# First batch of a Fourier-filter and swish kernel: spectrum rows turned ahead of the tables, masks and beta arithmetic on GpSimd with the filter loads behind them, one filter half copied on chip

## The chip, the cores and the metric

The kernel runs on one core of one Trainium2 chip. The metric is the device time of one execution in microseconds (us). The experiments ran in several sets of rounds on different chips, each set with the kernel before beside it (its medians are 804.01 to 804.79 us, its spread in one set 0.2 to 1.0%), so a ratio is taken inside a set, and medians of different sets are compared with care. "A gain" below means that the 95% interval of the ratio lies under 1.

## The reference, cut to what matters

```python
def _attn_ref(x, filt_r, filt_i):              # x: (8, 3008, 256); filters: (1505, 256)
    X = np.fft.rfft(x, axis=1)
    F = (filt_r + 1j * filt_i)[None, :, :]
    y = np.fft.irfft(X * F, n=x.shape[1], axis=1)
    return y.astype(np.float32)

def _moe_ref(x, w_in, w_out, beta):            # x: (24064, 256); d_ff = 2048
    h = x @ w_in
    g = h * (1.0 / (1.0 + np.exp(-beta * h)))
    return (g @ w_out).astype(np.float32)

# out = _moe_ref(_attn_ref(x, filt_r, filt_i).reshape(24064, 256), w_in, w_out, beta)
```

## The kernel before: the parts that matter

The transforms are matrix products with small tables. A long loop of steps (one step is one block of 512 tokens and one of 16 slices of d_ff) does h, silu and the output product. The transforms of batches 1 to 7 are placed between its steps. Batch 0 has nothing to hide behind: its transform and the building of the tables are the set-up, and the loop starts when the first slice of batch 0 is done.

The set-up, cut. `gp` is GpSimd. VectorE (DVE) multiplies the spectrum by the filters; rows 0 to 63 of `fr_sb` hold the real filter and rows 64 to 127 the imaginary one.

```python
for g in range(NG):                                    # 4 groups of 6 frequencies
    load_filter(fr_sb, filt_r, 0, g * KG, KG, nc.sync)
for g in range(2):
    load_filter(fr_sb, filt_i, M, g * KG, KG, gp)      # two DMAs of 192 KB each
ws = [load_wout(i * WG, WG) for i in range(2)]         # output weights, 512 KB each, from SyncE
# ... cut: first table, ka, kb ...
angles(0, nc.vector)
m_p = bits("m_p", ip[:], ALU.bitwise_and, M - 1)       # keep: the mask of the row of frequency 0
# ... cut: three more small VectorE instructions for keep ...
angles(1, gp)                                          # u, r, u - r: 128 x 768 fp32 each
for g in range(2, NG):
    load_filter(fr_sb, filt_i, M, g * KG, KG, gp)
for h in range(WI):
    gp.dma_start(win_sb[:, :, fs], moe_w_in[:, fs].rearrange(...))
# ... cut: first1 (x times the first table), table3 and turn_a (PE transposes) ...

def product(i):
    # ... cut: matmuls into ps, two of each ...
    for dst, ps in zip((p_t, q_t), pss):
        nc.vector.tensor_tensor(dst[:], ps[:], fr_sb[:, 2 * i : 2 * i + 2, :], ALU.mult)
```

In the loop, batches 1 to 7 need a second filter tile and the real filter in the rows where batch 0 had the imaginary one:

```python
def uf():
    units = []
    for f_sb, filt, at in ((fi_sb, filt_i, 0), (fi_sb, filt_i, M), (fr_sb, filt_r, M)):
        units += load_filter(f_sb, filt, at, 0, NK, nc.scalar, True)   # six DMAs of 768 KB
    units.append(lambda: gp.tensor_scalar_mul(fi_sb[:, 0, :], fi_sb[:, 0, :], keep[:]))
    return units
```

Batch 1's spectrum goes through DRAM: tile `a` is written to `d` (d<-a) and read back turned (a<-d). The read is placed at step 20 and its first matmul at step 26.

Of the kernel before, what the change touches and what calls it, by code (L numbers as in the profile page):

```python
# [9 lines left out]
P = 128  # L10

ACT = mybir.ActivationFunctionType
ALU = mybir.AluOpType
# [11 lines left out]
M = 64  # L25
H = M // 2
NK = 24
J = 32
KG = 6
NG = NK // KG  # L30
# [6 lines left out]
def kernel(  # L37
# [10 lines left out]
    nc = tc.nc  # L48
# [7 lines left out]
    NDC = D // P  # L56
    NFB = FF // P
# [62 lines left out]
    def load_filter(f_sb, filt, at, k0, n, eng, later=False):  # L120
        lo = AP(filt.tensor, filt.offset + k0 * D, [[N1 * D, H], [1, n * D]])
        hi = AP(filt.tensor, filt.offset + (N1 - k0) * D, [[N1 * D, H], [-D, n], [1, D]])
        units = [
            lambda: eng.dma_start(
                f_sb[at : at + H, k0 : k0 + n, :].rearrange("p k d -> p (k d)"), lo
            ),
            lambda: eng.dma_start(f_sb[at + H : at + M, k0 : k0 + n, :], hi),
        ]
        if later:
            return units  # L130
        for go in units:
            go()

    def load_wout(f0, n):
        ws = ostp.tile([P, n, D], F32, name="ws", tag="ost")
        nc.sync.dma_start(
            ws[:], moe_w_out[f0 * P : (f0 + n) * P, :].rearrange("(fb fp) j -> fp fb j", fp=P)
        )
        return ws
# [11 lines left out]
    def small(name, dt=F32):  # L151
        return setup.tile([P, 1], dt, name=name, tag=name)
# [6 lines left out]
    def bits(name, src, op0, s0, op1=None, s1=None):  # L159
        shape = [P, src.shape[1]]  # L160
        ti = setup.tile(shape, I32, name=name + "_i", tag=name + "_i")
        if op1 is None:
            nc.vector.tensor_scalar(ti[:], src, s0, None, op0)
        else:
            nc.vector.tensor_scalar(ti[:], src, s0, s1, op0, op1)
        tf = setup.tile(shape, F32, name=name, tag=name)
        nc.vector.tensor_copy(tf[:], ti[:])
        return tf
# [6 lines left out]
    def warm(n, cols=512):  # L175
        for _ in range(n):
            nc.tensor.matmul(pw[0][:, :cols], lhsT=wz[:, :P], rhs=wz[:, :cols], start=True, stop=True)

    ip = setup.tile([P, 1], I32, name="ip", tag="ip")
# [16 lines left out]

    for g in range(NG):
        load_filter(fr_sb, filt_r, 0, g * KG, KG, nc.sync)
    for g in range(2):
        load_filter(fr_sb, filt_i, M, g * KG, KG, gp)  # L200

    WG = NFB // 4
    ws = [load_wout(i * WG, WG) for i in range(2)]

    pre = small("pre")
    nc.scalar.activation(pre[:], wz[:, :1], ACT.Silu)
# [56 lines left out]
    def t2_part(h, part):  # L263
        u, r = us[h], rs[h]
        ks_ = slice(h * NH, (h + 1) * NH)
        if part == 0:
            nc.scalar.activation(t2[:, ks_, 2, :], u[:], ACT.Sin, scale=TWO_PI)
        elif part == 1:
            nc.scalar.activation(r[:], u[:], ACT.Abs)
        else:  # L270
            for cols, sgn, b in ((slice(0, H), -1.0, hp), (slice(H, M), 1.0, hm)):
                nc.scalar.activation(
                    t2[:, ks_, 1, cols], r[:, :, cols], ACT.Sin, scale=sgn * TWO_PI, bias=b[:]
                )

    def t2_neg(h):
        ks_ = slice(h * NH, (h + 1) * NH)
        nc.vector.tensor_scalar_mul(t2[:, ks_, 4, :], t2[:, ks_, 1, :], -1.0)
        nc.vector.tensor_copy(t2[:, ks_, 0, :], t2[:, ks_, 1, :])
        nc.vector.tensor_copy(t2[:, ks_, 3, :], t2[:, ks_, 2, :])  # L280

    angles(0, nc.vector)
    m_p = bits("m_p", ip[:], ALU.bitwise_and, M - 1)
    nc.vector.tensor_scalar(keep[:], m_p[:], -1.0, float(M - 1), ALU.mult, ALU.add)
    nc.vector.tensor_tensor(keep[:], keep[:], m_p[:], ALU.mult)
    nc.vector.tensor_scalar(keep[:], keep[:], 0.5, None, ALU.is_gt)

    angles(1, gp)
    for g in range(2, NG):
        load_filter(fr_sb, filt_i, M, g * KG, KG, gp)  # L290
    WI = 4
    for h in range(WI):
# [6 lines left out]
    def first1(i, on_act):  # L299
        for dc in range(NDC):  # L300
            if dc:
                ps = opsum.tile([P, 4, P], F32, name="psa", tag="acc")
            else:
                ps = fpsum.tile([P, 4, P], F32, name="psa", tag="f")
            for e in range(4):
                nc.tensor.matmul(
                    ps[:, e, :KP],
                    lhsT=x_cur[:, 4 * i + e, dc * P : (dc + 1) * P],
                    rhs=t1b[:],
                    start=True,  # L310
                    stop=True,
                )
            evac(
                a_t[:, dc, :, 4 * i : 4 * i + 4, :].rearrange("p k j a -> p j k a"),
                ps[:, :, :KP].rearrange("p j (k a) -> p j k a", a=4),
                on_act[dc],
            )

    for i in range(3):
        first1(i, (True, True))  # L320
        warm(2)
    t2_part(0, 0)
    first1(3, (False, True))
    warm(2)
    t2_part(0, 1)
    first1(4, (False, False))
    warm(2)
    t2_part(0, 2)
    first1(5, (False, False))
    warm(2)  # L330
    for i in range(6, 8):
        first1(i, (False, True))
        warm(2)
    t2_neg(0)



    def table3(i, part, on_act):
        pt = opsum.tile([P, KG, P], BF16, name="pt", tag="acc")
        for e in range(KG):  # L340
            nc.tensor.transpose(
                pt[:, e, :],
                t2[:, KG * i + e, part : part + 2, :].rearrange("p c k -> p (c k)"),
                ident[:],
            )
        dst = t3 if part else t3b
        if i == 0:
            evac(dst[:, 0, :], pt[:, 0, :], on_act, 0.5)
            evac(dst[:, 1:KG, :], pt[:, 1:KG, :], on_act)
        else:  # L350
            evac(dst[:, KG * i : KG * i + KG, :], pt[:], on_act)
# [14 lines left out]
                )  # L366
        evac(a2s[-1][:, 3 * (i % 2) : 3 * (i % 2) + 3, :], pb[:], on_act)

    table3(0, 0, False)
    turn_a(0, True)  # L370
    turn_a(1, False)
    table3(0, 2, True)

    nc.vector.tensor_scalar_mul(fr_sb[M:P, 0, :], fr_sb[M:P, 0, :], keep[M:P])


    def beta_columns():
        bps = hpsum.tile([P, NFB], F32, name="bps", tag="hps")
        id_f = setup.tile([NFB, NFB], F32, name="id_f", tag="id_f")
        nc.vector.tensor_copy(id_f[:], ident[:NFB, :NFB])  # L380
        nc.tensor.transpose(bps[:], bt[:], id_f[:])
        tiny = setup.tile([P, NFB], F32, name="tiny", tag="tiny")
        nc.vector.tensor_copy(beta_sb[:], bps[:])
        nc.vector.tensor_tensor(tiny[:], beta_sb[:], beta_sb[:], ALU.mult)
        nc.vector.tensor_scalar(tiny[:], tiny[:], 1e-12, None, ALU.is_lt)
        nc.vector.scalar_tensor_tensor(
            beta_sb[:], tiny[:], 2e-6, beta_sb[:], ALU.mult, ALU.add
        )
        nc.vector.reciprocal(rbeta_sb[:], beta_sb[:])
        nc.vector.tensor_copy(  # L390
            t1.rearrange("p (a k) -> p a k", a=4), t1b.rearrange("p (k a) -> p a k", a=4)
        )

# [54 lines left out]
    for i in range(NK // 2 + 1):  # L448
        if i < NK // 2:
            product(i)  # L450
        if i % 3 < 2 and i // 3 < 3:
            turn_a(2 + 2 * (i // 3) + i % 3, True)
        if i % 3 > 0 and i // 3 < 3:
            table3(1 + i // 3, 4 - 2 * (i % 3), True)
        if i in (1, 2, 3):
            t2_part(1, i - 1)
        if i == 2:
            beta_columns()
        if i == 3:
            t2_neg(1)  # L460
        if i == 9:
            table4()
        if i > 0:
            inverse3(i - 1)
# [37 lines left out]
    def last_z(g, i, on_act):  # L502
        jq, dc = divmod(i, NDC)
        yv = ys[0][:, dc, g * CLS : (g + 1) * CLS].rearrange("p (n j) -> p n j", j=JG)
        last4(zz0[g], t4b, 4 * jq, dc, yv[:, :, 4 * jq : 4 * jq + 4], on_act)
# [143 lines left out]
    def u4(b, act=False):  # L649
        return [lambda i=i: s4(b, i, act and i % 2 == 1) for i in range(J // 2)]  # L650

    def uz(g):
        return [lambda i=i: turn_z(g, i) for i in range(2)] + [
            lambda i=i: last_z(g, i, False) for i in range(2 * NDC)
        ]

    def uf():
        units = []
        for f_sb, filt, at in ((fi_sb, filt_i, 0), (fi_sb, filt_i, M), (fr_sb, filt_r, M)):
            units += load_filter(f_sb, filt, at, 0, NK, nc.scalar, True)  # L660
        units.append(lambda: gp.tensor_scalar_mul(fi_sb[:, 0, :], fi_sb[:, 0, :], keep[:]))
        return units

    def ux(b):
# [3 lines left out]
        return [go]  # L668

    place(1, 13, uz(1))  # L670
    place(1, 7, uf(), per=2)
    place(15, 29, uz(2))
    place(34, 60, uz(3))

    first_step = [(S * b // TB) * NFB for b in range(B + 1)]
    if B > 1:
# [130 lines left out]
```

## Time and profile before

The median is 803.98 us (three runs, 803.89 to 806.82). The span of the profiled run is 801.5 us.

| what | before |
|---|---|
| first spectrum product on VectorE | 19.35 us |
| first matmul of the loop | 43.39 us |
| PE's wait for the read of batch 1's spectrum | 73.2 to 76.15 us |
| from the loop's first matmul to the end of the span | 758.1 us |

The page of the kernel before, first the engines' busy time (share of the span, instructions), then the ACT queue's DMAs (packets, MB, share of the engines). PE is TensorE's matmuls, PEld its weight loads, DVE VectorE, ACT ScalarE, POOL GpSimd:

```profile
PE 774.1 (97%) x6007; PEld 547.9 (68%) x6103; DVE 408.8 (51%) x670; ACT 589.0 (73%) x896; POOL 149.9 (19%) x148
...
q10 hardware_dynamic: 2496, 4.72, 2.7%
```

PE is busy 97% of the span, so little is to be gained outside the few places where it is not. 4.72 MB on the ACT queue are the six filter loads.

The timeline of the kernel before (start and duration in us, engine, line, operation, tiles; in brackets the idle time of the engine before it and what ended it), GpSimd and VectorE in the set-up:

```profile
6.64 0.59 POOL L124 DMA_DIRECT2D fr_sb<-in_filt_i_dram  x1
...
10.28 1.48 POOL L252 TENSOR_TENSOR u<-ka,kb 128x768 f32<-128x768 f32 x1
...
14.73 1.80 POOL L259 TENSOR_TENSOR u<-u,r 128x768 f32<-128x768 f32 x1
...
15.05 1.69 DVE L278 TENSOR_SCALAR t<-t 128x768 bf16<-128x768 bf16 x1
...
16.67 0.35 DVE L279 COPY t<-t 128x768 bf16<-128x768 bf16 x1
...
18.91 0.35 DVE L374 TENSOR_SCALAR fr_sb<-fr_sb,keep 64x256 f32<-64x256 f32 x1
...
19.35 0.69 DVE L418 TENSOR_TENSOR pb_t<-ps,fr_sb 128x512 bf16<-128x512 f32 x1
```

The first group of the imaginary filter is issued at 6.64 us, ahead of the angles (10.28 to 16.53 us). VectorE's negation took 1.69 us while GpSimd's last angle instruction ran; the same instruction took 0.36 us at its second use. The products start at 19.35 us.

The timeline of PE at the start of the loop and at the read, in the kernel before:

```profile
43.39 1.02 PE L735 MATMUL hps<-y,win_sb 128*128 128x512 bf16 x4
...
76.15 0.39 PE L567 MATMUL ps<-a,t 128*128 128x256 bf16 x2 [2.89 <-DMA a<-d]
```

The windows view of the kernel before around that read (stretch, its length, then busy us and count of instructions of PE, PE's weight loads, DVE, ACT and POOL, then granted PE clock, DMA share, GB/s):

```profile
77.00:79.00 2.00, 2.00 (x9) 1.08 (x8) 1.65 (x3) 0.69 (x1) 0.20 (x1) 0.59 0.94 352
79.00:81.00 2.00, 2.00 (x12) 1.18 (x10) 1.47 (x3) 0.69 (x1) 1.06 (x1) 0.55 0.17 68
81.00:84.00 3.00, 2.95 (x26) 2.12 (x25) 2.71 (x5) 2.06 (x3) 1.27 (x1) 1.00 0.00 0
```

PE waited 2.89 us for the read, and its granted clock (the share of full speed that TensorE was given) was 0.59 and 0.55 from 77 to 81 us.

### The profile page before, as it was taken

How to read it: one execution, taken by the hardware profiler on the slowest of the kernel's cores; microseconds unless marked ns; L12 is line 12 of the kernel's file. 1: busy time of each engine (PE TensorE's matmuls, PEld its weight loads, DVE VectorE, ACT ScalarE, POOL GpSimd, SP SyncE). 2: the span in 40 equal slices, each digit the busy share in tenths (PEclk: the TensorE clock that was granted, in tenths of full speed). 3: DMA queues.
4: the chain of work that ended last, by engine and by line, in shares of the span. 5: the costliest groups of instructions: out<-in, count | busy, mean ns of one | idle time of the engine just before them, and what ended most of it. 6: DMA issues, size and time to landing. Idle time of an engine off the chain costs nothing.

```text
span 801.5 us, 15281 instructions
## 1 busy us (share of the span) xinstructions
PE 774.1 (97%) x6007; PEld 547.9 (68%) x6103; DVE 408.8 (51%) x670; ACT 589.0 (73%) x896; POOL 149.9 (19%) x148
## 2 busy tenths in 40 slices
PE   7798999999999999999999999999999999999997
PEld 4665667776677667776678766687667766776664
DVE  8874965574527655375644655357462770500001
ACT  5855776787677866788667886778767788677775
POOL 8531520240003300042001310023100340000000
PEclk9999999999999999999999999999999999999999
DMA  9999459323932167211870119502280115010101
GB/s 175 229 226 262 97 152 223 111 91 102 221 107 74 66 156 189 95 48 66 196 217 28 67 68 216 175 28 92 98 233 27 71 69 124 32 49 28 54 27 52
DMA packets 85890, 93.01 MB, mean 116 GB/s; under 512 B 3745, under 2 KB 76978, under 8 KB 84970
## 3 DMA queue, kind: packets, MB, share of 16 engines
q1 hardware_dynamic: 80250, 72.37, 30.6%
q0 software_dynamic: 3072, 14.94, 9.9%
q10 hardware_dynamic: 2496, 4.72, 2.7%
q8 instruction: 47, 0.77, 0.4%
q14 instruction: 25, 0.20, 0.1%
HBM read 58.73 MB, written 46.66 MB: 131 GB/s over the span
## 4 chain that ended last, share of the span: by engine, by line
PE 85%; DMA 6%; DVE 3%; issue 2%; ACT 2%; POOL 1%; DVEq 0%; ACTq 0%; POOLq 0%; SPq 0%
PE acc L763 39%; PE hps L735 35%; PE ps L545 3%; DMA d<-a 3%; PE ps L493 3%; PE ps L567 2%; PE ps L594 2%; DMA fr_sb<-in_filt_r_dram 2%; DVE ost L775 1%; DMA a<-d 1%; DMA xg<-in_x_dram 1%; ACT z_t L105 1%; ACT a L105 0%; DVE p_t L577 0%; DVE q_t L581 0%
## 5 line engine op out<-in xcount | busy, mean ns | idle before, releaser
L744 ACT ACTIVATE gT<-hps,beta_sb 128x512 bf16<-128x512 f32 x752 | 516.4, 687 | 192.3 <-PE hps L735 162.3
L763 PE MATMUL acc<-wout_sb,gT 128*128 128x256 bf16 x3008 | 456.4, 273 | 5.6 <-DVE ost L775 2.0
L735 PE MATMUL hps<-y,win_sb 128*128 128x512 bf16 (+7 forms) x1634 | 428.6, 351 | 0.5 <-ACT gT L744 0.4
L763 PEld LDWEIGHTS <-gT 128*128 128x128 bf16 x3008 | 285.7, 98 | 135.0 <-issue 6.2
L735 PEld LDWEIGHTS <-win_sb 128*128 128x128 bf16 x1728 | 164.7, 98 | 25.5 <-issue 0.9
L584 POOL TENSOR_TENSOR v_t<-p_t,q_t 128x512 bf16<-128x512 f32 x84 | 106.6, 1269 | 367.7 <-DVE q_t L581 365.5
L775 DVE COPY ost<-acc 128x512 f32<-128x512 f32 x94 | 60.3, 683 | 193.7 <-PE acc L763 193.6
L107 DVE CAST a<-ps 96x512 bf16<-96x512 f32 x104 | 71.0, 686 | 80.0 <-PE ps L545 79.9
L109 DVE TENSOR_SCALAR y<-ps 128x376 bf16<-128x376 f32 x126 | 68.8, 548 | 69.3 <-PE ps L493 69.0
L577 DVE TENSOR_TENSOR p_t<-ps,fr_sb 128x512 f32<-128x512 f32 x84 | 58.1, 691 | 32.1 <-PE ps L567 30.7
L581 DVE TENSOR_TENSOR q_t<-ps,fi_sb 64x512 f32<-64x512 f32 x84 | 58.2, 693 | 1.2
L578 DVE SCALAR_TENSOR_TENSOR q_t<-ps,fi_sb 64x512 f32<-64x512 f32 x84 | 57.4, 684 | 1.1
L493 PEld LDWEIGHTS <-zz 96*128 96x128 bf16 x512 | 35.5, 98 | 29.3 <-issue 0.6
L105 ACT ACTIVATE z<-ps 128x512 bf16<-128x512 f32 x84 | 49.4, 588 | 0.3 <-PE ps L594 0.2
L545 PE MATMUL ps<-xg,t 94*96 94x512 bf16 x112 | 42.1, 381 | 0.6
L493 PE MATMUL ps<-t,zz 96*128 96x94 bf16 x448 | 36.8, 206 | 1.0
L567 PE MATMUL ps<-a,t 128*128 128x256 bf16 x168 | 32.4, 275 | 3.5 <-DMA a<-d 3.1
L594 PE MATMUL ps<-v_t,t 128*128 128x256 bf16 x168 | 32.1, 273 | 0.2
L116 POOL DMA_DIRECT2D xg<-in_x_dram x12 | 6.9, 579 | 120.4 <-PE acc L763 97.8
L567 PEld LDWEIGHTS <-t 128*128 128x128 bf16 x168 | 15.9, 98 | 18.0 <-DMA a<-d 3.0
L545 PEld LDWEIGHTS <-t 94*96 94x96 bf16 x112 | 13.8, 124 | 12.0
L594 PEld LDWEIGHTS <-t 128*128 128x128 bf16 x168 | 15.5, 98 | 7.9 <-DVE q_t L581 0.7
(115 smaller groups left out, 196.7 us busy)
## 6 DMA issues: line engine op xcount, KB each, us to landing
out_dram<-ost SPq DMA_DIRECT2D x41, 512.0 KB, 3.0
d<-a SPq DMA_DIRECT2D x28, 384.0 KB, 6.7
a<-d SPq DMA_DIRECT2D x28, 384.0 KB, 5.4
d<-z SPq DMA_DIRECT2D x28, 384.0 KB, 3.2
zz<-d SPq DMA_DIRECT2D x28, 384.0 KB, 4.9
xg<-in_x_dram POOLq DMA_DIRECT2D x6, 1280.0 KB, 9.9
fi_sb<-in_filt_i_dram ACTq DMA_DIRECT2D x4, 768.0 KB
out_dram<-ost SPq DMA_DIRECT2D x20, 128.0 KB, 3.4
```

What stands on the lines that cost most here:

```text
L107: nc.vector.tensor_copy(dst, src)
L109: nc.vector.tensor_scalar_mul(dst, src, scale)
L493: nc.tensor.matmul(ps[:, e, :NP], lhsT=zz[:, jj + e, dc * P : (dc + 1) * P], rhs=tab[:], start=True, stop=True,)
L545: nc.tensor.matmul(ps[:KP], lhsT=t1[:], rhs=s["x"][:, 2 * i : 2 * i + 2, :], start=True, stop=True)
L567: nc.tensor.matmul(ps[:, e, :], lhsT=t2[:, k0 + e, 3:5, :].rearrange("p c k -> p (c k)"), rhs=s["a2"][g][:, kk + e, :], start=True, stop=True,
L581: nc.vector.tensor_tensor(q_t[:M], ps[M:P], fi_sb[M:P, k0 : k0 + 2, :], ALU.mult)
L584: nc.gpsimd.tensor_tensor(v_t[:], p_t[:], q_t[:], ALU.add)
L594: nc.tensor.matmul(ps[:, e, :], lhsT=t3[:, k0 + e, :], rhs=v_t[:, e, :], start=True, stop=True)
L735: nc.tensor.matmul(hps[:, pos - t0 : pos - t0 + ln], lhsT=win_sb[:, dc, fb * P : (fb + 1) * P], rhs=ys[b][:, dc, n0 : n0 + ln], start=(dc ...
L744: nc.scalar.activation(gT[:, :tn], hps[:, :tn], ACT.Silu, scale=beta_sb[:, fb : fb + 1])
L763: nc.tensor.matmul(acc[tb // 2][:, tb % 2, :], lhsT=gT[:, tb * P : (tb + 1) * P], rhs=wout_sb[:, fb, :], start=(fb == 0 and tb % 2 == 0), ...
L775: nc.vector.tensor_copy(ost[:, 2 * h : 2 * h + n, :], acc[h][:, :n, :])
```

## The change

The intent is twofold. In set-up, the rows of the spectrum are turned before the tables, and VectorE is relieved: masks and beta arithmetic go to GpSimd. For that GpSimd's order becomes masks, angles, then all eight imaginary-filter loads. In the loop, one filter load (two DMAs, 1.57 MB) gives way to four VectorE copies, `fr_sb` to `fi_sb`, since batch 0 already has that half on chip; the last quarter of batch 0's final stage is evacuated (copied out of PSUM) by ScalarE.

```diff
     for g in range(NG):
         load_filter(fr_sb, filt_r, 0, g * KG, KG, nc.sync)
-    for g in range(2):
-        load_filter(fr_sb, filt_i, M, g * KG, KG, gp)
     ws = [load_wout(i * WG, WG) for i in range(2)]
+    m_p = small("m_p")
+    gp.tensor_scalar(m_p[:], ip_f[:], float(M), float(-M), ALU.is_ge, ALU.mult)
+    gp.tensor_tensor(m_p[:], m_p[:], ip_f[:], ALU.add)
+    gp.tensor_scalar(keep[:], m_p[:], -1.0, float(M - 1), ALU.mult, ALU.add)
+    gp.tensor_tensor(keep[:], keep[:], m_p[:], ALU.mult)
+    gp.tensor_scalar(keep[:], keep[:], 0.5, None, ALU.is_gt)
...
     angles(0, nc.vector)
-    m_p = bits("m_p", ip[:], ALU.bitwise_and, M - 1)
-    nc.vector.tensor_scalar(keep[:], m_p[:], -1.0, float(M - 1), ALU.mult, ALU.add)
...
     angles(1, gp)
-    for g in range(2, NG):
+    for g in range(NG):
         load_filter(fr_sb, filt_i, M, g * KG, KG, gp)
...
-    table3(0, 0, False)
-    turn_a(0, True)
-    turn_a(1, False)
+    turn_a(0, False)
+    turn_a(1, True)
     table3(0, 2, True)
+    table3(0, 0, True)
+    t2_part(1, 2)
...
 (cut: first1 and the Sin instructions reordered; beta arithmetic from
  VectorE to GpSimd, the reciprocal of beta later; two t3b evacuations to VectorE)
...
-        for f_sb, filt, at in ((fi_sb, filt_i, 0), (fi_sb, filt_i, M), (fr_sb, filt_r, M)):
-            units += load_filter(f_sb, filt, at, 0, NK, nc.scalar, True)
-        units.append(lambda: gp.tensor_scalar_mul(fi_sb[:, 0, :], fi_sb[:, 0, :], keep[:]))
+        units = load_filter(fi_sb, filt_i, 0, 0, NK, nc.scalar, True)
+        for g in range(NG):
+            ks_ = slice(g * KG, (g + 1) * KG)
+            units.append(lambda ks_=ks_: nc.vector.tensor_copy(fi_sb[M:P, ks_], fr_sb[M:P, ks_]))
+        units += load_filter(fr_sb, filt_r, M, 0, NK, nc.scalar, True)
+        units.append(
+            lambda: nc.vector.tensor_scalar_mul(fi_sb[:M, 0, :], fi_sb[:M, 0, :], keep[:M])
+        )
...
-    place(1, 7, uf(), per=2)
+    place(1, 9, uf(), per=2)
-    place(34, 60, uz(3))
+    place(34, 60, uz(3, True))
```

More of the change, by code (lines that the diff above doesn't have):

```diff
@@ L274, in t2_part, with t2_more @@
                 )
-    def t2_neg(h):
+    def t2_more(h, eng):
         ks_ = slice(h * NH, (h + 1) * NH)
-        nc.vector.tensor_scalar_mul(t2[:, ks_, 4, :], t2[:, ks_, 1, :], -1.0)
-        nc.vector.tensor_copy(t2[:, ks_, 0, :], t2[:, ks_, 1, :])
-        nc.vector.tensor_copy(t2[:, ks_, 3, :], t2[:, ks_, 2, :])
+        eng.tensor_scalar_mul(t2[:, ks_, 4, :], t2[:, ks_, 1, :], -1.0)
+        eng.tensor_copy(t2[:, ks_, 3, :], t2[:, ks_, 2, :])
+        eng.tensor_copy(t2[:, ks_, 0, :], t2[:, ks_, 1, :])
     angles(0, nc.vector)
-    m_p = bits("m_p", ip[:], ALU.bitwise_and, M - 1)
-    nc.vector.tensor_scalar(keep[:], m_p[:], -1.0, float(M - 1), ALU.mult, ALU.add)
-    nc.vector.tensor_tensor(keep[:], keep[:], m_p[:], ALU.mult)
-    nc.vector.tensor_scalar(keep[:], keep[:], 0.5, None, ALU.is_gt)
     angles(1, gp)
-    for g in range(2, NG):
+    for g in range(NG):
         load_filter(fr_sb, filt_i, M, g * KG, KG, gp)
@@ L317, in first1 @@
             )
-    for i in range(3):
+    for i in range(2):
         first1(i, (True, True))
         warm(2)
-    t2_part(0, 0)
-    first1(3, (False, True))
-    warm(2)
-    t2_part(0, 1)
-    first1(4, (False, False))
-    warm(2)
-    t2_part(0, 2)
-    first1(5, (False, False))
-    warm(2)
-    for i in range(6, 8):
-        first1(i, (False, True))
-        warm(2)
-    t2_neg(0)
+    for part in range(3):
+        t2_part(0, part)
+    for i in range(2, 6):
+        first1(i, (False, False))
+        warm(2)
+    t2_more(0, nc.vector)
+    first1(6, (False, True))
+    warm(2)
+    for part in range(2):
+        t2_part(1, part)
+    first1(7, (False, False))
     def table3(i, part, on_act):
@@ L379, in beta_columns @@
         id_f = setup.tile([NFB, NFB], F32, name="id_f", tag="id_f")
-        nc.vector.tensor_copy(id_f[:], ident[:NFB, :NFB])
+        gp.tensor_copy(id_f[:], ident[:NFB, :NFB])
         nc.tensor.transpose(bps[:], bt[:], id_f[:])
@@ L383, in beta_columns @@
         nc.vector.tensor_copy(beta_sb[:], bps[:])
-        nc.vector.tensor_tensor(tiny[:], beta_sb[:], beta_sb[:], ALU.mult)
-        nc.vector.tensor_scalar(tiny[:], tiny[:], 1e-12, None, ALU.is_lt)
-        nc.vector.scalar_tensor_tensor(
-            beta_sb[:], tiny[:], 2e-6, beta_sb[:], ALU.mult, ALU.add
-        )
-        nc.vector.reciprocal(rbeta_sb[:], beta_sb[:])
-        nc.vector.tensor_copy(
+        gp.tensor_tensor(tiny[:], beta_sb[:], beta_sb[:], ALU.mult)
+        gp.tensor_scalar(tiny[:], tiny[:], 1e-12, 2e-6, ALU.is_lt, ALU.mult)
+        gp.tensor_tensor(beta_sb[:], beta_sb[:], tiny[:], ALU.add)
+        gp.tensor_copy(
             t1.rearrange("p (a k) -> p a k", a=4), t1b.rearrange("p (k a) -> p a k", a=4)
@@ L453 @@
         if i % 3 > 0 and i // 3 < 3:
-            table3(1 + i // 3, 4 - 2 * (i % 3), True)
-        if i in (1, 2, 3):
-            t2_part(1, i - 1)
+            table3(1 + i // 3, 4 - 2 * (i % 3), i % 3 == 1 or i < 3)
         if i == 2:
+            t2_more(1, nc.vector)
+        if i == 3:
             beta_columns()
-        if i == 3:
-            t2_neg(1)
+        if i == 7:
+            nc.vector.reciprocal(rbeta_sb[:], beta_sb[:])
         if i == 9:
@@ L650, in u4, with uz @@
         return [lambda i=i: s4(b, i, act and i % 2 == 1) for i in range(J // 2)]
-    def uz(g):
+    def uz(g, act=False):
         return [lambda i=i: turn_z(g, i) for i in range(2)] + [
-            lambda i=i: last_z(g, i, False) for i in range(2 * NDC)
+            lambda i=i: last_z(g, i, act) for i in range(2 * NDC)
         ]
     def uf():
-        units = []
-        for f_sb, filt, at in ((fi_sb, filt_i, 0), (fi_sb, filt_i, M), (fr_sb, filt_r, M)):
-            units += load_filter(f_sb, filt, at, 0, NK, nc.scalar, True)
-        units.append(lambda: gp.tensor_scalar_mul(fi_sb[:, 0, :], fi_sb[:, 0, :], keep[:]))
+        units = load_filter(fi_sb, filt_i, 0, 0, NK, nc.scalar, True)
[6 more added lines that the diff above has]
+        )
         return units
```

## The prediction

> **What bounds the kernel now.** The page gives PE 774 of 801.5 us busy (97%), so most of the span is out of reach. Two stretches are not PE-bound. (1) Until 43.4 us, where the first silu-loop matmul starts (timeline), batch 0 is transformed on chip; from 19.35 to 38.7 us VectorE is nearly back to back: 24 spectrum products at a 0.60 us step (14.5 us), about 1.5 us of beta work, a 1.2 us wait for the second table's Sin and its 0.9 us of copies. (2) At 73.2 us PE stops for about 3 us until batch 1's spectrum lands at 76.15 (who-waited view: PE for DMA a<-d), and the granted clock of 75 to 80 us is 0.74 (windows view). The chain of waits says why: filter load, then the d<-a write, then the read. From 44 to 72 us the DMA engines are near full; the ACT queue alone moves 4.7 MB of filters.
>
> **What the change does.**
> - It drops a 1.57 MB filter load after 44 us (six 768 KB issues become four) for four 64x1536 fp32 VectorE copies. At the 200 to 265 GB/s of those windows this is an estimated 6 to 7 us less DMA ahead of the d<-a writes. The copies, estimated at 0.9 to 1.7 us each (a 64x3072 bf16 VectorE instruction took 0.96), load VectorE by 4 to 7 us; a keep multiply on VectorE waits for a load.
> - Set-up: a 1.69 us VectorE negation (0.36 at its second use) beside a GpSimd instruction, the masks (0.6 us) and beta arithmetic (about 1 us) leave VectorE's path; Sins come earlier; two t3b evacuations (about 0.55 each) come to VectorE. But filt_i's first groups are issued after GpSimd's angles, at about 13.5 us instead of 6.6, so the first product may wait for its filter until 20 to 21 us.
> - The last quarter of batch 0's final stage goes from VectorE to ScalarE, where (80 to 107 us) VectorE is over 95% busy and PE waits 1.7 us for an ost copy.
>
> The Trainium skill, "SBUF — State Buffer" (Who interferes with whom), says that a two-port VectorE copy and a GpSimd instruction exclude each other; the 1.69 against 0.36 us agrees. The new copies fall beside GpSimd's wout scalings of 0.92 us. "TensorE: Matmul & The Clock Gate" (Part 1) says that an idle window drops PE to half clock; the 0.74 after the gap agrees, so closing the gap should return about 2 us of clock loss too.
>
> **Sum, estimates.** Set-up -1 (range -3 to +2); the 73 us stall and slow clock -5; VectorE congestion at 44 to 62 us +1.3; ost wait -0.5. Total -5.2 us, 0.65%.
>
> **Predicted: 798.8 us, 80% range 795 to 803.5.** Faster by over 2%: 0.02; within 2%: 0.97; slower by over 2%: 0.01.
>
> **What would show it.** First silu-loop matmul at 41 to 43.5 us; first product at 19 to 21 us, held by a filter DMA; no PE gap over 1 us at 70 to 77 us and clock 1.00 there; ACT queue 3.1 MB after 44 us; last d<-a landed before 68 us; VectorE near full from 44 to 60 us; from 120 us to the end the same length within 1 us.
>
> **What would make it wrong.** If VectorE falls behind by more than PSUM's three buffers hide, PE loses 3 us or more at 45 to 60 us, and the ScalarE queue, which waits for the copies before the filt_r load, delays silu. If filters arrive later than 21 us, set-up gets longer. If the a<-d read is late for another reason, the gain is near zero. If set-up is not filter-bound, the gain is up to 8 us.

## The result, and the profile after

The changed kernel's median is 804.03 us (four runs, 803.02 to 804.29); the kernel before, with one more run beside it, 804.16 us. The ratio is 0.9989, 95% interval 0.9966 to 1.0011: the same. Here and below a ratio is the mean time of one kernel's runs over that of the other's of the same rounds, so it is not quite the ratio of the medians quoted.

The unchanged total hides two large shifts, which the two profiles show:

| what | before | after | difference |
|---|---|---|---|
| first spectrum product | 19.35 | 26.20 | +6.85 |
| first matmul of the loop | 43.39 | 48.99 | +5.60 |
| from there to the end of the span | 758.1 | 753.4 | -4.7 |

The page of the changed kernel, the same two lines:

```profile
PE 781.1 (97%) x6101; PEld 550.6 (69%) x6101; DVE 411.2 (51%) x665; ACT 588.6 (73%) x896; POOL 154.5 (19%) x157
...
q10 hardware_dynamic: 1664, 3.15, 2.0%
```

The timeline of the changed kernel, GpSimd and VectorE in the set-up (columns as before):

```profile
6.73 0.68 POOL L204 TENSOR_SCALAR m_p<-ip_f 128x1 f32<-128x1 f32 x1
...
9.49 1.46 POOL L257 TENSOR_TENSOR u<-ka,kb 128x768 f32<-128x768 f32 x1
...
13.93 1.80 POOL L264 TENSOR_TENSOR u<-u,r 128x768 f32<-128x768 f32 x1
...
13.98 1.97 DVE L284 COPY t<-t 128x768 bf16<-128x768 bf16 x1
```

The same timeline further on, at the filter loads and the first product:

```profile
15.68 0.64 POOL L124 DMA_DIRECT2D fr_sb<-in_filt_i_dram  x1
...
25.75 0.35 DVE L373 TENSOR_SCALAR fr_sb<-fr_sb,keep 64x256 f32<-64x256 f32 x1 [6.96 <-DMA fr_sb<-in_filt_i_dram]
...
26.20 0.69 DVE L414 TENSOR_TENSOR pb_t<-ps,fr_sb 128x512 bf16<-128x512 f32 x1
```

Read it downward. The masks take GpSimd from 6.73 to 9.49 us. The angles end at 15.73 us, and only about then, at 15.68 us, is the first filter load issued, against 6.64 us before. VectorE then sits idle for 6.96 us before line 373, the mask multiply on `fr_sb`, and what ended the wait is the filter DMA. The slow VectorE instruction beside GpSimd's last angle instruction has not gone either: it is now the copy of 13.98 us, 1.97 us long. The whole loss lies ahead of the first product: from there to the loop it is 22.8 us, against 24.0 before.

The timeline of PE in the changed kernel:

```profile
48.99 1.02 PE L735 MATMUL hps<-y,win_sb 128*128 128x512 bf16 x4
...
78.70 0.38 PE L563 MATMUL ps<-a,t 128*128 128x256 bf16 x2
```

and the windows view of the changed kernel around the read:

```profile
70.00:75.00 5.00, 4.71 (x37) 3.12 (x35) 2.43 (x4) 3.18 (x5) 0.00 (x0) 1.00 0.75 199
75.00:80.00 5.00, 5.00 (x43) 3.56 (x41) 1.65 (x3) 3.44 (x5) 0.00 (x0) 1.00 0.96 329
```

No wait for the read is left, and the clock is 1.00. So the loop gave what was expected of it, and set-up took it back.

### The profile page after: what moved, and what is told of

Its sections match the earlier page's. It is cut to its first block, busy times and chain, and to the rows that moved or that the text cites. A ratio compares the mean times of both kernels' runs of the same rounds, so it can differ in the third digit from the quotient of the medians. Undisturbed runs are those within 1.5% of the kernel's fastest.

```text
span 802.4 us, 15376 instructions
## 1 busy us (share of the span) xinstructions
PE 781.1 (97%) x6101; PEld 550.6 (69%) x6101; DVE 411.2 (51%) x665; ACT 588.6 (73%) x896; POOL 154.5 (19%) x157
## 3 DMA queue, kind: packets, MB, share of 16 engines
q10 hardware_dynamic: 1664, 3.15, 2.0%
## 4 chain that ended last, share of the span: by engine, by line
PE 88%; DVE 4%; DMA 3%; POOL 2%; issue 2%; ACT 1%; DVEq 0%; POOLq 0%; SPq 0%; ACTq 0%
PE acc L763 39%; PE hps L735 38%; PE ps L541 3%; PE ps L489 2%; PE ps L563 2%; PE ps L590 2%; DMA d<-a 1%; DVE ost L775 1%; DMA fr_sb<-in_filt_i_dram 1%; PE psz L424 1%; DVE p_t L573 1%; DVE q_t L577 0%; DVE fi_sb L657 0%; DMA a<-d 0%; PE pz L481 0%
## 5 line engine op out<-in xcount | busy, mean ns | idle before, releaser
L735 PE MATMUL hps<-y,win_sb 128*128 128x512 bf16 (+7 forms) x1728 | 447.6, 351 | 0.0
L109 DVE TENSOR_SCALAR y<-ps 128x376 bf16<-128x376 f32 x122 | 66.6, 548 | 65.5 <-PE ps L489 65.2
```

The source lines that it names most:

```text
L109: nc.vector.tensor_scalar_mul(dst, src, scale)
L735: nc.tensor.matmul(hps[:, pos - t0 : pos - t0 + ln], lhsT=win_sb[:, dc, fb * P : (fb + 1) * P], rhs=ys[b][:, dc, n0 : n0 + ln], start=(dc ...
```

## The experiments

For each run the profile gives three numbers: the first product, the loop's start, and the time from there to the end.

| kernel | median us | ratio to before (95%) | first product | loop start | start to end |
|---|---|---|---|---|---|
| before | 804.16 | 1 | 19.35 | 43.39 | 758.1 |
| changed | 804.03 | 0.9989 (0.9966 to 1.0011) | 26.20 | 48.99 | 753.4 |
| e1_early_filter | 800.85 | 0.9947 (0.9929 to 0.9965) | 19.03 | 45.29 | 753.5 |
| e2_loop_only | 800.81 | 0.9959 (0.9938 to 0.9979) | 19.70 | 45.07 | 753.0 |
| e3_setup_only | 807.87 | 1.0039 (1.0024 to 1.0054) | 26.37 | 48.56 | 756.5 |
| e4_filter_on_sync | 799.54 | 0.9930 (0.9909 to 0.9950) | 20.70 | 43.46 | 754.5 |
| e5_sync_masks_late | 797.84 | 0.9941 (0.9909 to 0.9973) | 18.66 | 41.80 | 753.4 |
| e6_wout_after_filter | 800.95 | 0.9958 (0.9945 to 0.9971) | 23.20 | 45.39 | 753.4 |
| e7_copies_twice | 806.05 | 1.0019 (1.0006 to 1.0032) | 18.18 | 43.89 | 759.2 |
| e8_masks_last | 799.92 | 0.9943 (0.9930 to 0.9957) | 23.88 | 45.68 | 753.7 |
| e9_keep_pe_busy | 801.96 | 0.9960 (0.9925 to 0.9994) | 18.44 | 41.74 | 757.4 |
| e10_e5_again | 799.00 | 0.9948 (0.9912 to 0.9984) | 18.44 | 41.73 | 762.5 |
| e11_late_fi | 808.37 | 1.0029 (0.9984 to 1.0073) | 19.14 | 41.77 | 764.5 |
| e12_late_fi_early_wout | 809.57 | 1.0058 (1.0026 to 1.0091) | 19.60 | 51.06 | 756.5 |
| e13_both_behind | 802.40 | 0.9976 (0.9962 to 0.9990) | 24.68 | 46.48 | 753.7 |
| e14_first_group_early | 798.52 | 0.9929 (0.9914 to 0.9944) | 19.62 | 42.70 | 754.5 |

The last three columns come from one profiled execution each. The set-up code of before, e2 and e7 is the same, and its loop started at 43.39, 45.07 and 43.89 us: a difference of up to 1.7 us in a single profile proves nothing. Their first products came at 19.35, 19.70 and 18.18 us.

### The filter loads early again

```diff
+    for g in range(2):
+        load_filter(fr_sb, filt_i, M, g * KG, KG, gp)      # ahead of the masks and angles
...
-    for g in range(NG):
+    for g in range(2, NG):
         load_filter(fr_sb, filt_i, M, g * KG, KG, gp)
```

> The changed kernel, but the first two groups of the imaginary filter are issued where the kernel before issues them, ahead of the masks and angles on GpSimd. Theory (the late filter DMA holds the first product): first product at 18 to 20.5 us instead of 26.2, first silu-loop matmul at 42 to 44.5 us instead of 49.0, total 797 to 800 us. Rival A (masks, angles and beta work on GpSimd, or the reordering itself, lengthen set-up): first product moves by less than 2 us, total 802 us or more. Rival B (the stall at the spectrum read went away only because the loop started 5.6 us later): set-up recovers, but PE again waits 3 us or more for the read, total 802 to 804 us.

The first product came at 19.03 instead of 26.20 us and the total fell to 800.85 us, 0.85 us above the expected range. The timeline of GpSimd and VectorE in e1, at the middle angle instruction and at the first product:

```profile
13.29 2.81 POOL L265 TENSOR_SCALAR r<-u 128x768 f32<-128x768 f32 x1
...
14.25 0.35 DVE L286 COPY t<-t 128x768 bf16<-128x768 bf16 x1
...
19.03 0.69 DVE L416 TENSOR_TENSOR pb_t<-ps,fr_sb 128x512 bf16<-128x512 f32 x1 [0.89 <-DMA fr_sb<-in_filt_r_dram]
```

The loop started at 45.29 us, later than expected, because the angles now ended at 17.99 us and ScalarE, waiting 3.4 us for them, kept PE from the third product (2.7 us on VectorE). The rest of the loop was as in the changed kernel. So the late filter DMA is what held the first product, and rivals A and B fall as they were stated: the same masks and reordering did not hold the first product, and the stall did not come back. The masks are not free, though: behind the early loads they put off the angles, and the loop began 1.9 us later than in the kernel before, which is little more than the scatter of one profile.

### The two halves of the change, one at a time

e2: the kernel before, with the new `uf`, `place(1, 9, ...)` and `uz(3, True)` only. e3: the changed kernel, with those three undone.

> The kernel before with the loop part of the change alone: the four on-chip copies in place of the second filter load, and the last quarter of batch 0's final stage on ScalarE. Theory (1.57 MB less DMA ahead of the spectrum's writes): loop starts at 43.4 us as before, no PE gap over 1 us at the read, total 798 to 799.5 us. Rival B: the read still holds PE for 3 us, total 803 to 804 us. Rival C (the copies overload VectorE once the start is early): last write of the spectrum to DRAM is issued no earlier than before, gap of 1 to 3 us, total 800 to 803 us.

> The changed kernel with the loop part undone: the set-up part alone. Theory (set-up costs 5.6 us, and the loop part gains as much by itself): loop starts at 49 us, the stall at the read stays, total 808.5 to 810 us. Rival B (a later start by itself removes the stall): no gap over 1 us at the read, total 804 to 806 us.

By medians of the same rounds (804.41 us for the kernel before) the loop half gained 3.6 us and the set-up half cost 3.5 us; together -0.1 us, which is the whole change. e2's total is above the range expected (798 to 799.5 us), as its loop began at 45.07 us in the profile, but PE did not wait at the read. The timeline of PE in e2:

```profile
74.75 0.38 PE L567 MATMUL ps<-a,t 128*128 128x256 bf16 x2
```

The set-up half began its loop at 48.56 us and still had the stall. The timeline of PE in e3:

```profile
81.11 0.39 PE L563 MATMUL ps<-a,t 128*128 128x256 bf16 x2 [3.21 <-DMA a<-d]
```

The windows view of e3 during that wait and after it:

```profile
80.00:82.00 2.00, 0.89 (x8) 0.71 (x9) 0.46 (x1) 0.00 (x0) 0.00 (x0) 1.00 1.02 349
82.00:84.00 2.00, 2.00 (x16) 1.42 (x15) 1.91 (x4) 1.35 (x2) 0.25 (x1) 1.00 0.85 323
```

A later start by itself does not remove the wait (rival B falls again): 3.21 us were left. What removed it is the copies in place of one load, with the placement that goes with them; no run has these apart, and the other part of the loop half, the evacuation by ScalarE, comes later (step 34). That e3 cost 3.5 us and not the 5.2 us of its later start, and so missed the 808.5 to 810 us expected, is in part the clock: after this wait it stayed 1.00, while it fell to 0.55 in the kernel before. Counted by the starts of the loop's silu instructions (ACT gT), the steps from the 28th to the 33rd took 4.95 us against 6.62. Of these 1.7 us, 0.7 came back in the next eight steps, and the wait itself was 0.3 us longer. So only some 0.6 of the 1.6 us by which e3's loop part was shorter lies around the wait; 0.6 us lies ahead of it and 0.4 us behind the 61st silu, and one profile each cannot say why.

### The whole filter from SyncE

```diff
     for g in range(NG):
         load_filter(fr_sb, filt_r, 0, g * KG, KG, nc.sync)
+        load_filter(fr_sb, filt_i, M, g * KG, KG, nc.sync)
...
-    for g in range(NG):
-        load_filter(fr_sb, filt_i, M, g * KG, KG, gp)
```

> The changed kernel with the whole imaginary filter issued from SyncE, group by group beside the real one, so that GpSimd goes from masks to angles and needs no filter DMA. Theory: first product at 16.5 to 19.5 us, loop starts at 40 to 43 us, total 794.5 to 798.5 us, a gain over both kernels. Rival A (set-up is held by the GpSimd work): first product after 22 us, total over 800 us. Rival B: set-up recovers but the read stalls, total 800 to 804 us.

The total is 799.54 us, a gain over the kernel before, but the first product came only at 20.70 us; product, loop start and total are all later than expected. It no longer waited for a filter: VectorE's copy still took 1.97 us beside GpSimd's last angle instruction, and ScalarE waited 1.59 us for the angles.

### The masks behind the angles

Two kernels have the five mask instructions moved: e5, on the base of e4, directly behind the angles; e8, on the base of the changed kernel, behind the filter loads.

> The filter on SyncE (as in the run that did so) and the masks on GpSimd behind the angles instead of ahead of them. Theory: GpSimd ends the angles at about 13 us instead of 15.7, so VectorE's table copy no longer waits beside it (1.97 us becomes 0.35) and ScalarE no longer waits 1.6 us for the angles; first product at 18 to 19.5 us instead of 20.7, loop starts at 41 to 42.5 us instead of 43.5, total 796 to 799 us. Rival (the filter's landing is the next limit): first product at 20.5 us again, total unchanged within 0.5 us of 799.5.

> The changed kernel with the masks on GpSimd moved behind the filter loads. Theory (issue time and queue both hold the filter): the first filter load is issued at about 13 us instead of 15.7, the first product comes 1.5 to 2.8 us earlier (23.4 to 24.7 us), total 801 to 802.8 us. Rival (the DMA queue alone sets the landing): first product within 0.7 us of 26.2, total 803.5 to 804.5 us.

In e8 the first filter load was issued at 13.56 instead of 15.68 us and the first product came at 23.88 instead of 26.20 us: 2.1 us of issue gave 2.3 us at the product. The timeline of GpSimd and VectorE in e8:

```profile
13.56 0.63 POOL L124 DMA_DIRECT2D fr_sb<-in_filt_i_dram  x1
...
23.43 0.35 DVE L373 TENSOR_SCALAR fr_sb<-fr_sb,keep 64x256 f32<-64x256 f32 x1 [5.78 <-DMA fr_sb<-in_filt_i_dram]
```

The five instructions took 1.42 us there (18.13 to 19.55 us), where VectorE did not run its own angles; in the changed kernel 2.76 us, beside them. In both e5 and e8 VectorE's copy fell from 1.97 to 0.35 us, because the angles were over. e8's total is 799.92 us, 4.1 us below the changed kernel's (another set of rounds) and lower than expected; its six runs lie between 799.04 and 801.14 us. e5 came out as expected (first product 18.66 us, loop 41.80 us) and has the lowest median, but two of its six runs took 802.37 and 805.95 us; more on that below.

### The output weights behind the filter

```diff
-    ws = [load_wout(i * WG, WG) for i in range(2)]          # from SyncE
...
     for g in range(NG):
         load_filter(fr_sb, filt_i, M, g * KG, KG, gp)
+    ws = [load_wout(i * WG, WG, gp) for i in range(2)]      # from GpSimd
```

> The changed kernel with the first two output-weight loads (1 MB) issued from GpSimd behind the imaginary filter instead of from SyncE ahead of it. Theory (the filter lands late because 1 MB of output weights and the real filter are queued ahead and take most of the DMA until 24 us): first product at 22 to 24 us instead of 26.2, total 801 to 803 us. Rival (only the issue time counts): first product at 25.5 us or later, total 804 us.

The loads of the filter were issued at 15.68 us as in the changed kernel, and yet the first product came at 23.20 us, 3.0 us earlier; total 800.95 us, all six runs within 0.9 us. The rival, that only the issue time counts, falls. The timeline of VectorE in e6:

```profile
22.75 0.35 DVE L373 TENSOR_SCALAR fr_sb<-fr_sb,keep 64x256 f32<-64x256 f32 x1 [6.12 <-DMA fr_sb<-in_filt_i_dram]
```

The DMA queues between 17 and 21 us (queue, packets, MB, time of the packets as a share of the engines' time) in the changed kernel; q1 is SyncE's, q0 GpSimd's:

```profile
q1 hardware_dynamic: 786, 0.91, 108.6%
```

The same view of e6:

```profile
q0 software_dynamic: 146, 0.58, 66.6%
q1 hardware_dynamic: 236, 0.26, 35.1%
```

In the changed kernel nothing of GpSimd's queue moved in these 4 us, though its loads had been issued from 15.68 us on. In e6, with 1 MB less on SyncE's queue, most of what moved was the filter.

### The copies twice

```diff
-    nc.vector.tensor_copy(fi_sb[M:P, ks_], fr_sb[M:P, ks_])
+    [nc.vector.tensor_copy(fi_sb[M:P, ks_], fr_sb[M:P, ks_]) for _ in range(2)]   # base: e2
```

> The loop part of the change alone with each of its four VectorE copies made twice. Theory (VectorE's slack and the three PSUM buffers hide about 4 us of copies): at most 1 us over the loop part alone, total 800.5 to 802 us. Rival (each copy costs PE time): about 4 us more, total 804 to 805.5 us, and the spectrum's last write to DRAM is issued 3 us or more later, so that the read holds PE again.

Here the theory failed. The second four copies, about 1.05 us each, cost 5.2 us by medians (806.05 against 800.81 us for e2, from different rounds), more even than the rival said. The timeline of PE in e7:

```profile
53.26 0.38 PE L545 MATMUL ps<-xg,t 94*96 94x512 bf16 x1 [1.79 <-DVE a L107]
...
58.59 0.59 PE L545 MATMUL ps<-xg,t 94*96 94x512 bf16 x1 [3.05 <-DVE a L107]
```

PE waited 1.79 and 3.05 us for VectorE's evacuation of `a`, held behind the copies, and ScalarE waited 6.0 us for the copies before it could issue the real filter's load. From the loop's start to the first spectrum matmul e7 took 35.9 us (43.89 to 79.80), e2 29.7 us (45.07 to 74.75), and before 29.8 us to the point where PE stopped. PE did not wait for the read, so the rival's last sign failed. After the wait of 3.05 us the granted clock was 0.52 (58.5 to 60.5 us) and 0.63 (to 62.5 us), so the cost is not the copies' time alone. The four copies of the change cost nothing that these profiles show, but they use up VectorE's slack in that stretch; the next four cost more than their own time.

### Dummy matmuls, and the spread of e5

e9 adds ten dummy matmuls after the last `first1` of e5; e10 is e5 once more.

> The kernel with the filter on SyncE and the masks behind the angles, and ten dummy matmuls in the 2.3 us where PE waits for the last evacuation ahead of the turns; there the granted clock fell to 0.51 at 18 to 20 us. Theory: the clock stays at 1.00, the turns and first products of PE run in half the time, the loop starts 0.5 to 1.5 us earlier than at 41.8, total 796 to 797.5 us. Rival (set-up is by then paced by VectorE and the filters, not by PE's clock): clock 1.00, start and total unchanged within 0.5 us.

> The kernel with the filter on SyncE and the masks behind the angles once more, since its six runs spread from 797.0 to 806.0 us, and as the mate of the run with dummy matmuls on the same chip. Expected: median 797 to 799 us, a gain over the kernel before of 0.6 to 0.9 per cent.

With the dummy matmuls the granted clock at 18 to 20 us was 1.00 instead of 0.51, and the loop started at 41.74 instead of 41.80 us: so the loop's start agrees with the rival: PE's clock does not pace set-up here. Both kernels have the spread of e5 (e10: 796.69 to 805.95 us; e9: 797.33 to 805.98 us), so their medians say little. The profile of e10 is of its slowest run, and its timeline of PE shows where the time went, although the loop started at 41.73 us:

```profile
65.73 1.01 PE L762 MATMUL acc<-wout_sb,gT 128*128 128x256 bf16 x4 [4.47 <-POOL wout_sb L143]
```

PE waited 4.47 us for GpSimd's scaling of the output weights, which had waited 6.2 us for their load. In e5's own fast profile no such wait appears. In e10 PE waited 6.8 us for scalings in all, its clock was 0.50 for 4 us after the longest, and the 25th silu of the loop began 36.6 us after the first, against 27.6 in e5; from there on the two kernels' profiles agree within 0.1 us. So the 9.0 us between these two runs lie in the first 24 steps.

### Two attempts to mend e5

e11 moves the loop's first two filter loads from steps 1 and 2 to 7 and 8 and their mask to step 22. e12 adds to this the first output weights between the third and the fourth filter group on SyncE.

> The kernel with the filter on SyncE and the masks late, and in the loop the two loads of the imaginary filter's first half moved from steps 1 and 2 to steps 7 and 8, behind the copies, with its mask at step 22. Theory (its slow executions, 802 to 806 us, are those where the last output weights land late, because the filter loads share the DMA with them; the profile of one has PE wait 4.5 us for a GpSimd scaling at 65.7 us): no PE wait for a scaling over 0.5 us, all six runs within 3 us of each other, median 796 to 798 us. Rival (the late landing comes from the loads ahead of the loop, not from the filter loads in it): the spread stays, some runs over 802 us.

> As the run with the late filter loads, and the first two output-weight loads issued from SyncE behind the third and fourth filter group instead of both behind the fourth. Theory: the first weights land before 36 us, the scalings end earlier, all six runs within 3 us, median 795.5 to 798 us. Rival (the fourth filter group now comes late): products wait for a filter at about 31 us, loop starts 0.5 to 2 us later than 41.8, median 797.5 to 800 us.

Both are misses. The timeline of PE in e11:

```profile
68.66 1.01 PE L765 MATMUL acc<-wout_sb,gT 128*128 128x256 bf16 x4 [9.55 <-POOL wout_sb L143]
```

In e11 the last output weights came later still: the two filter loads were issued at 48.83 and 49.69 us and the last weights at 52.5 us, so the loads had been moved towards the ones that they were to avoid. The timeline of VectorE in e12:

```profile
39.97 0.69 DVE L415 TENSOR_TENSOR pb_t<-ps,fr_sb 128x512 bf16<-128x512 f32 x1 [5.93 <-DMA fr_sb<-in_filt_i_dram]
```

In e12 VectorE waited 5.9 us for the fourth filter group, which is the kind of wait that its rival named, and the loop started at 51.06 us, over 7 us later than the rival's range; PE's wait of 2.89 us for the read came back as well. What decides between e5's fast and slow executions stays open, but the traces show that the delay begins ahead of the loop, as e11's rival said: GpSimd's first scaling, which waits for the first weights, began at 36.32 us in e5, at 42.48 in e10 and at 41.63 in e11, before any filter load of the loop was issued (42.80 us in e10), and the last weights were issued at 45.9, 52.8 and 52.5 us.

### Both causes at once on GpSimd, and one group early

e13 puts masks and output weights behind the filter on GpSimd. e14 is e8 with the first of the four filter groups ahead of the angles:

```diff
     for g in range(NG):
         load_filter(fr_sb, filt_r, 0, g * KG, KG, nc.sync)
+    load_filter(fr_sb, filt_i, M, 0, KG, gp)
...
     angles(1, gp)
-    for g in range(NG):
+    for g in range(1, NG):
         load_filter(fr_sb, filt_i, M, g * KG, KG, gp)
+    (the five mask instructions)
```

> The changed kernel with both the masks and the first two output-weight loads on GpSimd behind the imaginary filter. Theory (issue time and queue add up): first filter load issued at about 13.5 us, first product at 19.5 to 21.5 us (26.2 in the changed kernel, 23.9 and 23.2 with one of the two), loop starts at 42.5 to 44 us, total 797 to 799.5 us. Rival (they overlap): first product at 23 us again, total about 800 us.

> The changed kernel with only the first group of the imaginary filter issued ahead of the angles, the other three behind them, and the masks behind those. Theory (the first product waits for one group only, and angles delayed by 1.2 us do little harm): first product at 18 to 19.5 us, a wait of up to 2 us for the second group, loop starts at 41.5 to 43.5 us, total 796 to 798.5 us. Rival (the second group lands as late as the first did, at 23 us or later, and holds products 4 to 6): loop starts at 44 us or later, total 799.5 us or more.

e13 decides nothing. The masks were queued behind the issue of the output weights, which itself waited for the filter, so VectorE now waited 6.6 us for the mask, not for a DMA; whether the two causes add up is open. e14 did nearly what was expected: first product at 19.62 us (0.1 late), loop at 42.70 us, 798.52 us (0.02 above the range), and all six runs between 798.47 and 798.97 us. It takes 0.9929 of the kernel before, its median is 5.5 us below the changed kernel's of another set of rounds, and it has none of e5's spread. The timeline of VectorE in e14 at its first product:

```profile
19.17 0.35 DVE L374 TENSOR_SCALAR fr_sb<-fr_sb,keep 64x256 f32<-64x256 f32 x1 [0.62 <-POOL keep L291]
19.62 0.69 DVE L415 TENSOR_TENSOR pb_t<-ps,fr_sb 128x512 bf16<-128x512 f32 x1
```

The timeline of PE in e14 at the start of its loop:

```profile
42.70 1.02 PE L736 MATMUL hps<-y,win_sb 128*128 128x512 bf16 x4
```

The last 0.62 us before the product are now the mask, not the filter.

## Why the prediction was right or wrong

- **"Set-up -1 (range -3 to +2)": wrong; this is the step that failed.** It measured +5.6 us in the profiles and +3.5 us by itself in e3, both outside the stated range. The mechanism had been seen ("the first product may wait for its filter until 20 to 21 us"), but two terms of that time were too small; how it came by them the prediction does not show. The issue was put at "about 13.5 us"; it was 15.68. e8, with no masks ahead of the loads, issued at 13.56 us (product at 23.88), so the figure left no room for the masks on GpSimd, which took 2.76 us there; the prediction has them only as 0.6 us off VectorE's path. The landing, by its own times, was put some 7 us after the issue; it took 10 (15.68 to 25.75 us). In e6, with 1 MB of output weights taken off SyncE's queue, it took 7.1 (15.68 to 22.75 us; product at 23.20). What the real filter on the same queue adds, no run shows. With the filter early (e1) the product was back at 19.03 us.
- **"A 1.69 us VectorE negation leaves VectorE's path": wrong.** The wait beside GpSimd's last angle instruction moved to the next copy and was 1.97 us. It went where no VectorE copy fell beside that instruction: the angles ended earlier in e5 and e8 (0.35 us), later in e1 (0.35 us). That a two-port VectorE instruction and a GpSimd one shut each other out is what the Trainium skill, "SBUF — State Buffer" (Who interferes with whom), states. But it was not so for every GpSimd instruction here: the copy of e1 shown above took 0.35 us beside GpSimd's middle angle instruction, a tensor_scalar.
- **"The 73 us stall and slow clock -5": right in mechanism and about right in size.** The loop and the rest were 4.7 us shorter, with the other two loop terms in it; the predicted sum of the three was -4.2. e2 alone gained 3.6 us by medians. By the silu starts of the two profiles, the stall's steps (25th to 28th) took 6.06 us before and 2.99 after, the steps of the slow clock (to the 33rd) 6.62 and 4.95; but the next eight took 10.29 and 11.21, so that 0.9 of these 4.7 us was given back. From the 61st silu to the end it is 681.8 and 681.5 us. The clock part is not certain, though: e3 had a longer wait and no clock loss. "TensorE: Matmul & The Clock Gate" (What's actually happening) calls the activity window free-running, so that the place of a wait in it would count too; a wait of 2.89 us with a loss and one of 3.21 us without fit that, but no run shows the window.
- **"VectorE congestion +1.3": too high; the copies cost about nothing**, as e2's 29.7 us against 29.8 show, and the first 24 steps, 27.4 us both before and after. But e7 shows that there was no room for more.
- **"ost wait -0.5": agrees.** The longest wait of PE for that copy (of the output out of PSUM) went from 1.73 us before to 1.05 us, and the 20 steps around it (41st to 61st silu) from 25.3 to 24.7 us; no run had this part alone.
- Of the signs to look for: no PE gap and a clock of 1.00 at 70 to 77 us, 3.15 MB on the ACT queue, the same length from about 120 us to the end, and a VectorE nearly full at the start of the loop (15.45 of its first 17 us, against 12.76 before), came true, as did a first product held by a filter DMA. The times of the first product (26.2 us) and of the loop's start (49.0) did not, and the last d<-a was issued at 69.9 us, because all began later.

So 798.8 us was wrong by 5.2 us, nearly all of it set-up (4.5 us by e3's median); 804.03 us lies 0.5 us above the stated range. The chances of a change over 2% were judged rightly.

## What to carry to other kernels

Work moved to an idle engine also moves everything queued behind it on that engine; if the engine issues DMAs, count when the first of them now leaves and what is already queued ahead of it in the other queues. A transfer that the first consumer needs should be issued ahead of the moved work, even if it is only one group of it (e14). And a total that does not move is no sign that nothing happened: compare the stretches of the two profiles, and run each half alone.

## What the Trainium skill lacked or had wrong

- "DMA: Bandwidth & Descriptors" (Queues, rings and completion order) says that each DMA engine takes packets from its queues in turn. No even sharing could be planned on that: from 17 to 21 us GpSimd's queue moved nothing in the changed kernel while SyncE's moved 0.9 MB, although GpSimd's loads had been issued from 15.68 us on; with 1 MB less on SyncE's queue (e6) GpSimd's moved more than SyncE's in the same 4 us. The page has nothing on how long a queue's start is held back by another's backlog; whether arbitration or descriptor writing did it, no run shows. (VectorE was idle from 18.8 to 25.75 us, so its instructions do not explain it.)
- "TensorE: Matmul & The Clock Gate" (Part 1) gives one idle window of about 3.4 us as what halves the clock. Here a wait of 2.89 us was followed by 0.55 to 0.59, one of 2.34 us (e5, ahead of the turns) by 0.51 and one of 3.05 us (e7) by 0.52, while one of 3.21 us (e3) was followed by 1.00: waits shorter than that window were followed by a lower clock, and the length of a gap alone did not tell.
- "GPSIMD Engine Reference" (Elementwise — side-by-side cycle accounting) gives GpSimd about twice VectorE's time for a long tensor_tensor; here one of 128x768 took 1.48 to 1.80 us on GpSimd and 0.96 on VectorE (before). It lacks very small instructions and their neighbours: five 128x1 instructions took 0.9 us on VectorE (9.13 to 10.03 us, before), 1.42 us on GpSimd in e8, and 2.76 us in the changed kernel beside VectorE's angles.
- "SBUF — State Buffer" (Who interferes with whom) says that the engine which comes second is fully blocked. That agreed beside GpSimd's last angle instruction, a tensor_tensor: 1.97 against 0.35 us for the same VectorE copy. Beside its middle one, a tensor_scalar of 2.81 us, copies of the same size took 0.35 us in e1 and e6. Spans on GpSimd are rough in a profile, so this is an observation and not yet a rule.
